# Softmax of the first batch with tokens on partitions, and another order of the opening, in an attention and MLP kernel on one core

## The chip, the cores and the metric

The kernel runs on one core of a Trainium2 chip. The metric is the device time of one execution in microseconds. Five engines work side by side, each through a queue of its own in order: TensorE (PE, matrix products into the PSUM memory), VectorE (DVE), ScalarE (ACT), GpSimd (POOL) and SyncE (SP), which here issues the loads. An instruction waits at the head of its queue until semaphores say that its inputs and its buffer are ready, and everything behind it in that queue waits too.

## The reference, cut to what matters

```python
def _attn_ref(q, k, v, phi):          # q, k, v: 8 x 8 x 576 x 64, phi: 8 x 8 x 576 x 32
    a = phi - np.max(phi, axis=2, keepdims=True)
    a = np.exp(a)
    a = a / (np.sum(a, axis=2, keepdims=True) + 1e-09)
    k_m = np.einsum('bhsm,bhsd->bhmd', a, k)
    v_m = np.einsum('bhsm,bhsd->bhmd', a, v)
    scores = scale * np.matmul(q, k_m.transpose(0, 1, 3, 2))
    scores = scores - np.max(scores, axis=-1, keepdims=True)
    attn = np.exp(scores)
    attn = attn / (np.sum(attn, axis=-1, keepdims=True) + 1e-09)
    return np.matmul(attn, v_m)
def _moe_ref(x, w_in, w_out):         # x: 4608 x 512, w_in: 512 x 2048, w_out: 2048 x 512
    h = x @ w_in
    g = h - np.tanh(h)
    return g @ w_out
```

Each of the 8 batches has 8 heads with a memory of 32 rows: `k_m` and `v_m` are 32 x 64 for each head, and the softmax of a token runs over 32 scores for each head. The weights come as 64-bit floats.

## The kernel before, in words

**Staging.** The product `attn @ v_m @ w_in` is taken as `attn @ P`, where `P = v_m @ w_in` is made once for each batch and each of four blocks `fb` of 512 columns of `w_in` (the word `P`, function `att_p`). The 4608 tokens are cut into 18 units `u` of 256. For each unit and block, `mm1` (word `H`, L723) makes `h` from `P` and the weights of attention, a row of elementwise steps makes `g` from `h`, and `mm2` (word `M`, L804) or `mm2_blocks` multiplies `g` by `w_out`. Precision comes from pairs of 16-bit numbers: each factor is split into a high and a low half (`ph` and the second half of its tile for P, which `att_pl` makes, `ah` and `al` for the attention weights, `win_hi` and `win_lo`, `wout_hi` and `wout_lo`), and each product is taken from three of the four combinations, so `mm1` takes 24 products for one unit of one batch.

**The weights.** `conv` (word `T`) turns a pair of 64-bit blocks into 32-bit floats: `tops` (the upper bits, `to_tops`, L524), then a shift and or on VectorE (`to_f32`, L532, tiles `wq` or `wt` by pair: pair 0 is `wq0`), then the high half (L564). `low` (`L`) or `low_pe` (`Lp`, a product on TensorE, tile `pw`) makes the low half. `P` of block 0 needs pairs 0 and 1, of block 1 pairs 2 and 3. The pair's raw blocks are `raw0` and `raw1`, and so on; blocks from 16 on are of `w_out`.

**Batch 0.** The scores are made with the 32 rows of the memory of 4 heads on the 128 partitions and the tokens along the columns (`scores`, L394, two tiles `t` of 288 tokens). VectorE turns them in squares of 32 by 32 (L403), so that a token's 32 scores lie along the columns; maximum (L422), difference (L424, on GpSimd), exponential (L427), sum (L433 to L435) and division (L437) follow, and VectorE turns the result back (L442) for the split into `ah` and `al` (`att_split`). `kT` is the turned `k_m`, `kvn` the pooled and normalised memory, `vh` and `vl` the halves of the turned `v_m`.

**Order.** All that happens until unit 4 stands in a table of words, `START`. Each word is a step or, for a function with `yield`, its next part; a word thus issues a few instructions, and the table fixes the order in every queue. `Z` issues two products on constant data that nobody reads (`warm`). `ENGINES` and `PLACES` give some steps to another engine or buffer. From unit 4 on a planner's slots follow. PSUM buffers are scarce: tag `pa` has one, tag `h` two; a tile of `pp` (P before its split) takes the `pa` buffer.

## Time and profile before

| what | value |
|---|---|
| runs | 640.74, 641.08, 643.17 us; median 641.08 us |
| the profiled execution | 641.09 us, of which the profile spans 639.3 us |
| TensorE products | 627.8 us busy, 98% of the span |
| VectorE, ScalarE, GpSimd | 523.9, 367.3, 260.7 us busy |

Busy time is a sum over engines that work at once, so the table says only which of them has no room left. The `warm` products are in TensorE's busy time too.

### The profile page before, as it was taken

The numbers are of one execution on the slowest core, as the hardware profiler recorded it, in microseconds if no ns is written. First come the engines' busy times: TensorE is split into PE (matmuls) and PEld (weight loads), VectorE is DVE, ScalarE is ACT, GpSimd is POOL, SyncE is SP. The second block draws the span as 40 slices with busy tenths as digits, with TensorE's granted clock in tenths as the row PEclk, the third lists the DMA queues.
The fourth block names the chain that finished last, engine by engine and source line by source line (L and its number), as shares of the span: only waits on it lengthen the run. The fifth ranks groups of instructions, "written<-read, shape, count | busy, mean of one in ns | idle before, by whom it ended". The sixth has DMA issues, their size and how long they took to land.

```text
span 639.3 us, 15482 instructions
## 1 busy us (share of the span) xinstructions
PE 627.8 (98%) x6658; PEld 453.3 (71%) x6658; DVE 523.9 (82%) x755; ACT 367.3 (57%) x491; POOL 260.7 (41%) x179
## 2 busy tenths in 40 slices
...
GB/s 322 377 415 319 274 55 249 38 150 122 48 63 105 169 3 89 44 159 149 108 79 115 173 87 62 153 174 36 107 158 141 100 111 121 87 101 124 87 35 38
DMA packets 28156, 85.50 MB, mean 134 GB/s; under 512 B 3632, under 2 KB 4400, under 8 KB 27568
## 3 DMA queue, kind: packets, MB, share of 16 engines
...
q14 instruction: 22, 0.18, 0.1%
...
## 4 chain that ended last, share of the span: by engine, by line
PE 70%; DVE 9%; issue 7%; ACT 6%; POOL 4%; DMA 1%; SPq 0%; ACTq 0%; POOLq 0%; DVEq 0%
PE hs L723 16%; PE x L870 11%; PE o L863 9%; PE o L804 9%; PE o L870 7%; PE h L723 7%; PE o1h L804 3%; DVE f L772 3%; PE pp L684 3%; PE pkv L354 2%; ACT u L730 2%; POOL g L759 2%; DVE h L748 2%; DVE h L738 2%; DMA raws<-in_w_in_dram 1%
## 5 line engine op out<-in xcount | busy, mean ns | idle before, releaser
L759 POOL TENSOR_TENSOR g<-h,g 128x1024 f16<-128x1024 f32 x64 | 140.9, 2202 | 301.6 <-ACT g L114 174.7
L723 PEld LDWEIGHTS <-ph 128*128 128x128 f16 x2304 | 177.6, 98 | 20.2 <-issue 4.1
L723 PE MATMUL hs<-ah,ph 128*128 128x256 f16 (+3 forms) x1152 | 151.4, 246 | 0.0
L723 PE MATMUL hs<-al,ph 128*128 128x256 f16 (+3 forms) x576 | 127.6, 246 | 0.0
L743 ACT ACTIVATE u<-u,beta 128x1024 f32<-128x1024 f32 x72 | 82.5, 1148 | 76.3 <-DVE h L738 76.3
L114 ACT ACTIVATE g<-h 128x1024 f16<-128x1024 f32 x64 | 67.6, 1056 | 101.1 <-DVE h L748 97.1
L738 DVE SCALAR_TENSOR_TENSOR h<-hs,u 128x1024 f32<-128x1024 f32 x54 | 65.8, 1219 | 72.9 <-ACT u L730 72.1
L863 PE MATMUL o<-wout_hi,g 128*128 128x512 f16 x432 | 104.6, 379 | 0.0
L870 PEld LDWEIGHTS <-f 128*128 128x128 f16 x896 | 87.7, 98 | 10.1
L748 DVE SCALAR_TENSOR_TENSOR h<-u,h 128x1024 f32<-128x1024 f32 x72 | 88.4, 1228 | 4.5 <-ACT u L743 4.4
L870 PEld LDWEIGHTS <-g 128*128 128x128 f16 x672 | 64.2, 98 | 27.3 <-issue 6.0
L870 PE MATMUL x<-bt,f 128*128 128x256 f16 x672 | 82.5, 273 | 0.0
L804 PEld LDWEIGHTS <-g 128*128 128x128 f16 x384 | 36.7, 98 | 47.2 <-issue 2.6
L863 PEld LDWEIGHTS <-g 128*128 128x128 f16 x432 | 41.2, 98 | 40.1 <-issue 3.8
L772 DVE TENSOR_TENSOR f<-g 128x512 f16<-128x512 f16 x112 | 68.3, 650 | 1.7
L730 ACT ACTIVATE u<-hs 128x1024 f32<-128x1024 f32 x54 | 54.8, 1016 | 23.1 <-PE hs L723 20.4
L804 PE MATMUL o<-wout_hi,g 128*128 128x512 f16 x192 | 58.8, 379 | 0.6 <-ACT g L114 0.6
L723 PE MATMUL h<-ah,ph 128*128 128x256 f16 (+3 forms) x384 | 50.4, 246 | 0.7 <-DVE ph L702 0.7
L723 PE MATMUL h<-al,ph 128*128 128x256 f16 (+2 forms) x192 | 42.5, 246 | 0.0
L804 PE MATMUL o<-wout_lo,g 128*128 128x512 f16 x96 | 36.4, 379 | 0.0
L599 POOL TENSOR_TENSOR fy<-chk 128x512 f32<-128x512 f32 x32 | 33.7, 1067 | 0.0
L870 PE MATMUL o<-bt,g 128*128 128x256 f16 x224 | 33.6, 273 | 0.0
...
## 6 DMA issues: line engine op xcount, KB each, us to landing
...
```

The lines of the kernel that those rows point to most:

```text
L114: nc.scalar.activation(o, x, AF.Copy, scale=1.0 if scale is None else scale)
L599: nc.gpsimd.tensor_tensor(y, hf, hf, op=ALU.mult)
L723: nc.tensor.matmul(hp[:, k, tu : tu + w], px[:, g, cs], d[ax][:, g, ta : ta + w], start=(n == 0), stop=(n == 5),)
L730: nc.scalar.activation(uu, hp, AF.Square, scale=1.0 / (S_A * S_P))
L738: nc.vector.scalar_tensor_tensor(h3, hp, C2 * S_G / (S_A * S_P), uu, op0=ALU.mult, op1=ALU.mult)
L743: nc.scalar.activation(uu, uu, AF.Square, bias=c["beta"])
L748: nc.vector.scalar_tensor_tensor(h3, uu, CC, hp, op0=ALU.add, op1=ALU.mult)
L759: (eng or on(nc, f"gl{u}_{fb}", "g")).tensor_tensor(gg[:, 1], h3, gg[:, 0], op=ALU.subtract)
L772: nc.vector.tensor_tensor(o, x, y, op=op)
L804: nc.tensor.matmul(o, gx[:, k, P * tt : P * tt + P], wx[:, 4 * fb + k, :], start=(first and k == 0 and wx is wout_hi and gx is gh), stop=( ...
L863: nc.tensor.matmul(o[th], gg[:, 0, k, P * th : P * th + P], wout_hi[:, 4 * fb + k, :], start=(first and k == 0), stop=False)
L870: nc.tensor.matmul(dst, a(1 - n, kk), b(n, kk), start=(new and kk == 0 and n == 0), stop=(end and kk == 1 and n == 1))
```

## The change

For batch 0 alone the scores come out with tokens on the partitions (`rows_scores`): the queries of a head are the stationary factor, 128 tokens at a time, and the moving factor is `k2`, a tile of 64 columns for each head in which the memories of the two heads of a pair stand in two diagonal blocks. Tile 0 holds 512 columns (tokens 0 to 255), tile 1 holds 640. The two turns on VectorE before and the two behind the softmax are gone: maximum and difference (both on VectorE now) read PSUM, the division is on VectorE, and TensorE turns the weights (`rows_turn`) into PSUM, from where `ah` and `al` are made. The queries of batch 0 come in another layout from the host (`qa`).

P of batch 0, blocks 0 and 1, is made from 32-bit factors in one go (`p_exact`: 8 products in place of 24); it needs neither the low halves nor the high ones. `v_m` is kept in 32 bits for that (`vT0`).

`START` stands in another order, and steps of the first units change engines and buffers. `conv` issues shift and high half one word earlier. Three more `Z` stand in the table. The diff, cut:

```diff
 START = """
-FX0 KK01 KK00 XR00 XR01 Z00 YX00 YX01 XT00 i4:kv2 Q00 XT00 Q01 KV00 XT01 XT01 XT01 Z00 VK00 KV01 VK01 i3:gg i2:gg NK0
...
+FX0 Z00 XR00 XR01 YX00 XT00 YX01 KK01 Z00 XT01 Z00 XT00 KK00 i2:gg XT01 XT01 i3:gg Q00 VK00 VK01 Q01 NK0 T01 Z00 Z00
...
 ENGINE_LIST = """
-g: hi11 lo10 lo11 lo12 lo13 lo14 lo4 lo5 lo6 lo8 sc11 sc14 tops13 tops2 tops8
-v: ah21 al00 al10 al21 div10 div20 e01 e10 el0 gh0_3 gh1_2 gh1_3 gh2_1 gh2_2 gh3_1 gh3_2 gh4_0 gl0_0 gl0_1 gl0_2
...
+g: hi1 hi12 hi6 lo1 lo10 lo11 lo12 lo13 lo14 lo5 lo6 lo7 sc11 sc14 sc6 sc7 tops1 tops11 tops13 tops15 tops3 tops8
+v: ah20 al10 al21 div00 div01 div10 div11 div20 e01 e10 el0 gh1_2 gh1_3 gh2_3 gh3_1 gh4_0 gh4_1 gl0_0 gl1_2 gl1_3
...
 PLACE_LIST = """
-0: raw18 g11 g03 h340
...
+2: g31
 """
...
+EXACT = tuple((0, fb) for fb in (0, 1,))
...
         yield
-        d["kT"] = self.big.tile([P, 128], F32, tag="kT", name="kT0", bufs=1)
-        cast(self.tc, self.c, "kT0", "a", d["kT"], pa)
+        k2, pa = self.k2, pa.rearrange("p (h m) -> p h m", m=32)
+        cast(self.tc, self.c, "kT0", "a", k2[0:64, :, 0], pa[0:64])
+        nc.vector.tensor_copy(k2[64:P, :, 1], pa[64:P])
...
-        self.tc.nc.sync.dma_start(x, self.ins["qt"][b, t])
+        self.tc.nc.sync.dma_start(x, self.ins["qt"][b, t] if b else self.ins["qa"][t])
...
+    def rows_scores(self, d, t, ps):
+
+        nc, k2 = self.tc.nc, self.k2
+        pa = ps[0].tile([P, 512], F32, tag="o1", name="psc00") if t == 0 else self.psum("psc01", ps[1]).rearrange("p a x -> p (a x)")
+        d["ps", t] = pa
+        for c in range(2):
+            px = pa[:, 256 * c : 256 * c + 256].rearrange("p (r h m) -> p h r m", r=2, h=4)
+            for h in range(4):
+                nc.tensor.matmul(px[:, h], d["q", h, t][:, P * c : P * c + P], k2[:, h], start=True, stop=True)
+        if t == 0:
+            return
+        for j in range(2):
+            for r in range(2):
+                rs, os = slice(64 * r, 64 * r + 64), slice(64 * r + 32 * j, 64 * r + 32 * j + 32)
+                for h in range(4):
+                    nc.tensor.matmul(
+                        pa[os, 512 + 32 * h : 544 + 32 * h], d["q", h, j][rs, 256:HS], k2[rs, h, r], start=True, stop=True
+                    )
+
+    def rows_max(self, d, t):
+
+        nc, big, n, o = self.tc.nc, self.big, (512, 640)[t], 512 * t
+        if t == 0:
+            d["sc"] = big.tile([P, S * 2], F32, tag="sc", name="sc0")
+        p3 = d["ps", t][:, 0:n].rearrange("p (n m) -> p n m", m=32)
+        d["s", t] = s = d["sc"][:, o : o + n]
+        d["s3", t] = s3 = s.rearrange("p (n m) -> p n m", m=32)
+        m = big.tile([P, n // 32], F32, tag="sm", name=f"sm0{t}")
+        nc.vector.tensor_reduce(m, p3, axis=AX.X, op=ALU.max)
+        yield
+        nc.vector.tensor_tensor(s3, p3, m.unsqueeze(2).to_broadcast((P, n // 32, 32)), op=ALU.subtract)
+
+    def rows_turn(self, d, t, ps):
+
+        nc, s, ident = self.tc.nc, d["s", t], self.c["ident"]
+        if t == 0:
+            pa = ps[0].tile([P, 512], F32, tag="o1", name="pat0").rearrange("p (r x) -> p r x", r=2)
+        else:
+            pa = self.psum("pat1", ps[1])
+        for c in range(2):
+            for r in range(2):
+                o = 256 * c + P * r
+                nc.tensor.transpose(pa[:, r, P * c : P * c + P], s[:, o : o + P], ident)
+        for r in range(2 * t):
+            rs = slice(64 * r, 64 * r + 64)
+            nc.tensor.matmul(pa[:, r, 256:320], s[rs, 512:640], ident[rs, rs], start=True, stop=True)
+        d["ps", t] = pa[:, :, 0 : 256 + 64 * t]
...
-        nc, NB, s3 = self.tc.nc, HS // 16, d["s3", t]
+        nc, s3 = self.tc.nc, d["s3", t]
+        NB = HS // 16 if b else 16 + 4 * t
...
+    att.k2 = big.tile([P, 4, 2, 32], F32, tag="kvn", name="k2")
+    nc.gpsimd.memset(att.k2, 0)
...
         to_f32(p, y, ts)
+        t = ts[0].bitcast(F32).rearrange("p (i f) -> p i f", i=2) if len(ts) == 1 else None
+        tfs[p] = [t[:, i] for i in range(2)] if len(ts) == 1 else [t.bitcast(F32) for t in ts]
         tops.append(y)
         yield
-        yield
         his[p] = half_of(p, win_hi, wout_hi)
-        if len(ts) == 1:
-            t = ts[0].bitcast(F32).rearrange("p (i f) -> p i f", i=2)
-            tfs[p], todo = [t[:, i] for i in range(2)], [(his[p], t)]
-        else:
-            tfs[p] = [t.bitcast(F32) for t in ts]
-            todo = [(his[p][:, i], tfs[p][i]) for i in range(2)]
+        todo = [(his[p], t)] if len(ts) == 1 else [(his[p][:, i], tfs[p][i]) for i in range(2)]
         for o, x in todo:
...
         pv = d["pv"]
-        d["vh"] = big.tile([P, 128], F16, tag="vh", name=f"vh{b}", bufs=3)
-        d["vl"] = big.tile([P, 128], F16, tag="vl", name=f"vl{b}", bufs=3)
         d["p"] = [None] * NFB
+        if b == 0:
+            d["v"] = big.tile([P, 128], F32, tag="vT", name="vT0", bufs=1)
+            cast(tc, c, "vf0", "a", d["v"], pv)
+            yield
+        d["vh"] = big.tile([P, 128], F16, tag="vh", name=f"vh{b}", bufs=2)
+        d["vl"] = big.tile([P, 128], F16, tag="vl", name=f"vl{b}", bufs=2)
         cast(tc, c, f"vh{b}", "a", d["vh"], pv, S_V)
         yield
...
+        if b == 0:
+            ts, pa = slice(256 * t, 256 + 320 * t), d["ps", t]
+            nc.scalar.activation(d["ah"][:, :, ts], pa, AF.Copy)
+            yield
+            nc.vector.tensor_tensor(d["al"][:, :, ts], pa, d["ah"][:, :, ts], op=ALU.subtract)
+            return
...
+
+    def p_exact(fb, pa):
+        for h in range(4):
+            w = tfs[2 * fb + h // 2][h % 2]
+            for r in range(2):
+                rs = slice(64 * r, 64 * r + 64)
+                nc.tensor.matmul(
+                    pa[32 * h : 32 * h + 32, r, :], st[0]["v"][rs, 32 * h : 32 * h + 32], w[rs], start=True, stop=True
+                )
+
+    def p_scale(b, fb):
+        return S_P if (b, fb) in EXACT else S_P / (S_V * S_W)
...
-        p_terms(b, fb, pa, True)
+        p_exact(fb, pa) if (b, fb) in EXACT else p_terms(b, fb, pa, True)
...
         pp = big.tile([P, 2, 2, 512], F16, tag=P_TAG[b, fb], name=f"ph{b}{fb}", bufs=1)
...
-        cast(tc, c, f"ph{b}{fb}", "a", ph, pa, sc)
+        cast(tc, c, f"ph{b}{fb}", "a", ph, pa, p_scale(b, fb))
...
-        nc.vector.scalar_tensor_tensor(pl, pa, S_P / (S_V * S_W), ph, op0=ALU.mult, op1=ALU.subtract)
+        nc.vector.scalar_tensor_tensor(pl, pa, p_scale(b, fb), ph, op0=ALU.mult, op1=ALU.subtract)
...
-        if u == 0:
-            ots = big.tile([P, 2, DM], F32, tag="uu", name=f"ot{u}")
         for tt in range(2):
-            ot = ots[:, tt] if u == 0 else pr.tile([P, DM], F32, tag="pr", name=f"ot{u}{tt}")
+            ot = pr.tile([P, DM], F32, tag="pr", name=f"ot{u}{tt}")
...
-        "S": lambda b, t: att.scores(b, st[b], t, early(b) if t or b == 0 else None),
-        "AM": lambda b, t: att.soft_max(b, st[b], t), "AE": lambda b, t: att.soft_exp(b, st[b], t), "AD": lambda b, t: att.soft_div(b, st[b], t, S_A),
-        "AT": lambda b, t: att.soft_turn(b, st[b], t), "AS": att_split,
+        "S": lambda b, t: att.scores(b, st[b], t, early(b) if t or b == 0 else None) if b else att.rows_scores(st[0], t, (ps_o, ps_early)),
+        "AM": lambda b, t: att.soft_max(b, st[b], t) if b else att.rows_max(st[0], t), "AE": lambda b, t: att.soft_exp(b, st[b], t), "AD": lambda b, t: att.soft_div(b, st[b], t, S_A),
+        "AT": lambda b, t: att.soft_turn(b, st[b], t) if b else att.rows_turn(st[0], t, (ps_o, ps_early)), "AS": att_split,
...
+    qa = q[0].reshape(4, 2, S, D).transpose(1, 3, 0, 2).reshape(P, 4, S)
+    qa = np.stack([np.concatenate([qa[:, :, 256 * t : 256 * t + 256], qa[:, :, 512 + 32 * t : 544 + 32 * t]], axis=2) for t in range(2)])
```

**What moves.** The first place is ScalarE's queue behind the first exponential of batch 0 (`sc0` are the scores, `vy` sums for a check on the range, `vT0` the 32-bit copy of `v_m`). Before:

```order
L427 ACTIVATE sc0_238<-sc0_238 128x576
L114 ACTIVATE win_hi_101<-wt20_253 128x512
L114 ACTIVATE win_hi_101<-wt21_254 128x512
L427 ACTIVATE sc0_238<-sc0_238 128x576
L114 ACTIVATE tops1_107<-raw2_211 128x512
L114 ACTIVATE tops1_107<-raw3_209 128x512
L114 ACTIVATE tops0_105<-raw0_218 128x512
L114 ACTIVATE tops0_105<-raw1_220 128x512
L114 ACTIVATE vh0_355<-pk0_167 128x128
L114 ACTIVATE ah0_362<-af0_335 128x2x288
```

Now:

```order
L477 ACTIVATE sc0_270<-sc0_270 128x512
L477 ACTIVATE sc0_270<-sc0_270 128x640
L717 ACTIVATE vy00_341,stat_67<-kvn0_214 128x64
L717 ACTIVATE vy01_343,stat_67<-kvn0_214 128x64
L115 ACTIVATE tops1_109<-raws4_294 128x1024
L727 ACTIVATE ah0_360<-pat0_354 128x2x256
L115 ACTIVATE vT0_363<-pk0_168 128x128
L115 ACTIVATE win_hi_101<-wt20_387 128x512
```

The two exponentials follow each other; behind them come the sums for the check, the upper bits of pair 2 (`raws4`), the first `ah` and then `vT0`. In VectorE's queue the cast to `vh0` now waits for `vT0` and stands ahead of the second division.

The second place is VectorE's queue from the conversion of pair 1 (before) and from the second division (now) to the split of the first P (the line that writes `ph00`). Before:

```order
L532 SCALAR_TENSOR_TENSOR wq1_338<-raw2_211,tops1_107 128x512
L532 SCALAR_TENSOR_TENSOR wq1_338<-raw3_209,tops1_107 128x512
L442 STREAM_TRANSPOSE af0_335<-sc0_238 128x576
L532 SCALAR_TENSOR_TENSOR wq0_352<-raw0_218,tops0_105 128x512
L532 SCALAR_TENSOR_TENSOR wq0_352<-raw1_220,tops0_105 128x512
L118 TENSOR_SCALAR win_hi_101<-wq1_338 128x512 x2
L658 SCALAR_TENSOR_TENSOR vl0_356<-pk0_167,vh0_355 128x128
L584 SCALAR_TENSOR_TENSOR win_lo_102<-wq1_338,win_hi_101 128x512 x2
L532 SCALAR_TENSOR_TENSOR wq3_377<-raws6_239,tops0_105 128x1024
L118 TENSOR_SCALAR win_hi_101<-wq3_377 128x2x512
L675 TENSOR_TENSOR al0_363<-af0_335,ah0_362 128x2x288
L702 SCALAR_TENSOR_TENSOR ph00_420<-pp00_387,ph00_420 128x1024
```

Now:

```order
L488 TENSOR_TENSOR sc0_270<-sc0_270,sz01_350 128x640
L711 SCALAR_TENSOR_TENSOR vl0_374<-pk0_168,vh0_373 128x128
L585 SCALAR_TENSOR_TENSOR wt20_387<-raws4_294,tops1_109 128x512
L585 SCALAR_TENSOR_TENSOR wt21_388<-raws4_294,tops1_109 128x512
L117 CAST tops0_107<-raw0_297 128x512
L117 CAST tops0_107<-raw1_306 128x512
L585 SCALAR_TENSOR_TENSOR wq0_401<-raw0_297,tops0_107 128x512
L585 SCALAR_TENSOR_TENSOR wq0_401<-raw1_306,tops0_107 128x512
L729 TENSOR_TENSOR al0_361<-pat0_354,ah0_360 128x2x256
L729 TENSOR_TENSOR al0_361<-pat1_379,ah0_360 128x2x320
L772 SCALAR_TENSOR_TENSOR ph00_420<-pp00_406,ph00_420 128x1024
L585 SCALAR_TENSOR_TENSOR wq3_423<-raws6_331,tops1_109 128x1024
```

Pair 0 (`wq0`) now stands behind the whole softmax, behind pair 2 (`wt20`, `wt21`) and behind its own two `tops` casts, which ScalarE made before. `wq3` (pair 3) now stands behind the split of the first P.

The third place is TensorE's queue ahead of the first product of unit 0 (`h00`). Before:

```order
L684 LDWEIGHTS vh0_355
L684 MATMUL pp00_387<-win_lo_102,vh0_355 32x512
L590 MATMUL pw3_424<-wq3_377,idw_63 128x512
L591 LDWEIGHTS nid16_65
L591 MATMUL pw3_424<-win_hi_101,nid16_65 128x512
L590 MATMUL pw3_424<-wq3_377,idw_63 128x512
L591 LDWEIGHTS nid16_65
L591 MATMUL pw3_424<-win_hi_101,nid16_65 128x512
L723 LDWEIGHTS ph00_420
L723 MATMUL h00_451<-ah0_362,ph00_420 128x256
```

Now:

```order
L640 MATMUL pw0_429<-win_hi_101,nid16_65 128x512
L1036 LDWEIGHTS w16_66
L1036 MATMUL warm_111<-w16_66 128x512
L1036 LDWEIGHTS w16_66
L1036 MATMUL warm_111<-w16_66 128x512
L741 MATMUL pp01_445<-wt20_387,vT0_363 32x512 x2
L741 MATMUL pp01_445<-wt21_388,vT0_363 32x512 x2
L741 MATMUL pp01_445<-wq3_423,vT0_363 32x512 x4
L793 LDWEIGHTS ph00_420
L793 MATMUL h00_454<-ah0_360,ph00_420 128x256
```

Ahead of `h00` stood a low half, `pw3`, and now stands the second P, `pp01`, whose last four products read `wq3`. `pw3` now follows `h00`. `pp01` shares a PSUM buffer with `pp00`, and so it waits until `ph00` is split in full.

## Rows read from the trace of the kernel before

**Rows 1.** Timeline of TensorE, opening: start us, busy us, engine, line, instruction, count, [idle before].
```profile
7.32 0.63 PE L334 MATMUL pet<-ident,pt 128*128 128x128 f32 x4 [1.01 <-issue]
7.88 0.43 PE L335 MATMUL pel<-ident,pt 128*64 128x128 f32 x2
...
9.19 0.60 PE L968 MATMUL warm<-w 128*128 128x512 f16 x2
...
10.33 0.32 PE L208 MATMUL pk<-kt,e 64*32 64x65 f32 x8
...
13.26 0.72 PE L394 MATMUL psc<-q,kT 64*32 64x288 f32 x16 [0.57 <-DMA q<-in_qt_dram]
```

**Rows 2.** The same timeline, where the main products of the first units start.
```profile
28.70 1.13 PE L590 MATMUL pw<-wq,idw 128*128 128x512 f32 x2
...
31.02 0.27 PE L723 MATMUL h<-ah,ph 128*128 128x256 f16 x1
...
32.05 0.39 PE L723 MATMUL h<-ah,ph 128*128 128x256 f16 x2 [0.65 <-DVE ph L702]
...
34.56 0.41 PE L684 MATMUL pp<-win_hi,vh 64*32 64x512 f16 x8
...
40.93 1.98 PE L354 MATMUL pkv<-kv,e 128*32 128x129 f32 x64 [0.51 <-ACT e L114]
```

**Rows 3.** The chain that ended last, one link: start us, us, what.
```profile
35.40 2.73 PE h L723 x24
```

**Rows 4.** Timeline of TensorE at two later places.
```profile
82.61 0.39 PE L804 MATMUL o<-wout_hi,g 128*128 128x512 f16 x1 [0.56 <-ACT g L114]
...
184.09 0.23 PE L723 MATMUL hs<-ah,ph 128*128 128x128 f16 x1
```

**Rows 5.** Stretches: PE, PEld, DVE, ACT, POOL busy (instructions), PE clock, DMA share, GB/s.
```profile
15.00:16.00 1.00, 1.00 (x17) 0.13 (x2) 0.97 (x3) 0.00 (x0) 0.00 (x0) 0.50 1.03 399
200.00:300.00 100.00, 100.00 (x1114) 76.78 (x1112) 74.53 (x120) 50.27 (x66) 35.65 (x21) 1.00 0.28 98
```

**Rows 6.** Groups by line: busy us, mean ns of one.
```profile
L334 PE MATMUL pet<-ident,pt 128*128 128x128 f32 x16 | 2.6, 282 | 1.0 <-issue 1.0
...
L442 DVE STREAM_TRANSPOSE af<-sc 128x576 f32<-128x576 f32 x16 | 12.3, 767 | 0.0
...
L403 DVE STREAM_TRANSPOSE sc<-psc 128x576 f32<-128x576 f32 x12 | 9.2, 770 | 0.6 <-PE psc L394 0.6
```

**Rows 7.** Timeline of VectorE.
```profile
17.99 0.75 DVE L433 TENSOR_REDUCE sz<-sc 128x18 f32<-128x576 f32 x1 [0.49 <-ACT sc L427]
...
21.45 0.25 DVE L217 TENSOR_TENSOR kvn<-pk,kr 128x128 f32<-128x128 f32 x1
21.62 1.72 DVE L532 SCALAR_TENSOR_TENSOR wq<-raw,tops 128x512 uint32<-128x512 uint32 x2
...
23.96 1.25 DVE L532 SCALAR_TENSOR_TENSOR wq<-raw,tops 128x512 uint32<-128x512 uint32 x2
...
30.78 1.21 DVE L702 SCALAR_TENSOR_TENSOR ph<-pp,ph 128x1024 f16<-128x1024 f32 x1
...
34.44 0.80 DVE L116 CAST tops<-raw 128x512 f16<-128x512 bf16 x2
```

**Rows 8.** Timeline of ScalarE.
```profile
12.72 0.28 ACT L114 ACTIVATE kT<-ptr 128x128 f32<-128x128 f32 x1 [4.14 <-PE ptr L224]
...
18.90 0.67 ACT L427 ACTIVATE sc<-sc 128x576 f32<-128x576 f32 x1
...
23.22 0.78 ACT L114 ACTIVATE tops<-raw 128x512 f16<-128x512 bf16 x1 [0.49 <-DMA raw<-in_w_in_dram]
...
25.79 1.35 ACT L114 ACTIVATE tops<-raws 128x1024 f16<-128x1024 bf16 x1
...
28.84 1.02 ACT L114 ACTIVATE ph<-pp 128x1024 f16<-128x1024 f32 x1
...
51.07 0.24 ACT L664 ACTIVATE vy<-kvn 128x64 f32<-128x64 f32 x1
```

More of the change, by code (lines that the diff above doesn't have):

```diff
@@ new lines @@
+Z00 UU0 o6:gg W0 o7:gg Z00 AD00 AD01 AT00 T02 AS00 UV0 Z00 Z00 FX1 o0:gg UV0 Z00 AD01 AT01 UV0 T02 T02 Lp02 AS01 T00
+T00 T00 P00 AS00 T01 AS01 T03 P00 PL00 T03 XR10 Z00 Lp00 T11 Lp00 T11 T11 Z00 P01 H00 T03 P01 Lp02 KB1 H00 XR11 L11
+o1:gg KA1 YX10 o2:gg YX11 o3:gg T08 PL01 Lp03 XT10 T08 XT11 Lp03 XT10 ap00 H10 XT11 XT11 V10 V11 L01 T08 H10 ap00 a10
+H11 L01 i10:kv3 Q10 ap00 T09 N1 U1 o4:gg T09 a10 o5:gg H01 T09 Q11 ap00 a10 L09 i8:kv2 UV1 L09 L08 U1 T05 UV1 H11 S10
+T10 H01 L08 c00 S10 T10 a10 T05 T10 L11 a11 AM10 a11 L10 i14:kv3 M00 c10 AM10 ap01 Q20 S11 L10 M10 FA2 a11 ap01 S11
```

41 lines of the change are left out of this document (18 added, 23 removed).

## The prediction

> **What bounds the kernel now.** I read the totals first: TensorE is busy 98% of the span, no other engine above 82%. Then the stretches: between 200 and 300 us TensorE has no gap, at the full granted clock, in the last of [rows 5]. Then TensorE's timeline for its gaps. Ahead of 32.05 us there are many waits; behind, only two that belong to this change's stretch: 0.51 us ahead of the first product for batch 1's memory at 40.93 [rows 2], and 0.56 us at 82.61 [rows 4]. The chain of waits agrees: from the first product of `h` it is mostly TensorE itself [rows 3]. So the end of the kernel is the start of `h00`, plus TensorE's work behind it. From 184.09 on (unit 4) [rows 4] both kernels follow the same list of slots; what counts happens before.
>
> **The sum's frame.** I call X the time at which `h00` starts and runs through. Before, two of its 24 products ran early at 31.02 and the rest from 32.05 [rows 2]; a link of 24 takes 2.73 [rows 3], so one takes 0.11, and X was 32.05 - 0.22 = 31.83. Behind `h00` the change takes from TensorE: `pp01` (34.56 to 35.40, 0.8) [rows 2, 3]; two `warm` products, 0.6 as the pair at 9.19 [rows 1]; the 0.51 at 40.93, since batch 1's memory and another product of `h` have changed places; and, if the new order also covers it, the 0.56 at 82.61. It adds `pw3`, which now follows `h00`: the first half of such a low half starts at 28.70, and the four products end at 31.02 [rows 2], so 2.3. Net: 0.8 + 0.6 + 0.51 + 0.56 - 2.3 = 0.2 us less work. So the kernel is as fast as before if X is 31.83 + 0.2 = 32.0, and every microsecond of X beyond is one of time.
>
> **What the change removes.** On the path to `h00` stood two turns from PSUM and two back, 0.77 each [rows 6], and subtraction and division on GpSimd. It also removes three low or high halves ahead of P. But in its place stands a new chain, which I now walk.
>
> **Scores.** `kT` was ready at 12.72 + 0.28 = 13.00 [rows 8] and the queries let the scores start at 13.26 [rows 1]. Now a further `warm` pair (0.6) lies ahead on TensorE, and the second half of `k2` is a copy on VectorE, priced as the small `kvn` step, 0.25 [rows 7], and partly beside ScalarE's half. I take 13.95 (bounds 13.3 and 14.2). Each tile takes 8 products in 32-bit with 128 stationary columns and 64 moving; a 32-bit product leaves two records, so 16. Before, a stationary factor was 32 columns wide, four products lay side by side, and 16 records took 0.72 [rows 1]. The new ones fill the array and cannot lie side by side. The nearest rows are the turns `pet`: four records of 128 by 128 in 32-bit, 0.63 in all with 0.282 for one [rows 1, 6], so (0.63 - 0.282) / 3 = 0.116 from one to the next. That makes 16 x 0.116 = 1.86 for a tile: `psc00` ends at 15.8. The lower bound is 256 column-passes at full clock, 0.11 for a product as in `h` [rows 3], so 0.9 a tile; the upper one is a pair of `pel` at 0.43 [rows 1], so 3.4. I choose the middle one, being the same size of stationary factor and type. `psc01` has the same plus 16 small products, about 0.06 each (eight records at 10.33 take 0.32) [rows 1]: 2.9, ending at 18.8.
>
> **Softmax.** VectorE's price is 0.75 for 576 columns [rows 7], so 0.67 for tile 0 and 0.83 for tile 1. The chain behind 18.8: maximum 1 to 19.7, then (it stands ahead in the queue) sum 0 and its small steps 1.2, to 20.9; difference 1 to 21.8; exponential 1 on ScalarE, 0.74 from 0.67 [rows 8], to 22.55. On ScalarE follow two sums for the check (0.24 each [rows 8], with their waits 0.7) to 23.25, upper bits of pair 2, 1.35 [rows 8], to 24.6, `ah` 0.6 to 25.2, `vT0` 0.28 to 25.5. `vh0` on VectorE waits for `vT0`, though division 1, right behind it in the queue, was ready: 0.25 to 25.75. What is queued behind this wait is division 1 and the whole of pair 2, then pair 0.
>
> **From there to P.** Division 1, 0.83, `vl0` 0.25, pair 2 1.25 [rows 7], the two `tops` casts 0.80, `wq0` 1.25 [rows 7]: 30.15. Independent neighbours on VectorE overlap by some 0.08 (one row ends at 21.70, and the next starts at 21.62 [rows 7]), over seven of them 0.6: `wq0` ends at 29.5. Before, it ended at 25.2 [rows 7]. `pp00` from 32-bit factors: a 32-bit product of 512 columns takes about 0.9 (1.13 less the 0.2 by which a lone row outlasts its spacing [rows 2]); the eight lie side by side, as the eight of `pp` do, which also take 0.41 [rows 2]. So 30.4. Then `ph` 1.02 [rows 8] to 31.45, and `pl` 1.21 [rows 7] to 32.7.
>
> **The new wait.** `pp01` stands ahead of `h00` in TensorE's queue. It needs `pp00`'s buffer, free at 32.7, and `wq3`, which stands behind `pl` on VectorE: 1.2 as a conversion of 1024 columns (two of 512 take 1.25 [rows 7]), so 33.85. Its last four products take 0.9: **X = 34.8**, 2.8 later than the break-even of 32.0. `pw3` behind `h00` waits for the eviction of `pw2` on ScalarE, two evictions of 1.02 [rows 8] after `pp01`, and is hidden by `h00`'s 2.7.
>
> **Costed at nothing.** GpSimd gets some 12 us more work up to unit 4 and VectorE loses 6; the cover is TensorE, full behind `h00`, and half of GpSimd's time is idle. The queue of SP: its load of a later block of `w_out` waits for `wq0`'s buffer and holds the loads behind it back by 1 to 2 us; unit 0's second stage, which needs them, has some 17 us of products ahead of it. If that cover is gone, up to 1 us. The clock: it fell to 0.50 between 15 and 16 us, after a pause in the scores [rows 5], and I count no such fall for the new scores, since nothing interrupts the two tiles.
>
> [...] The turn from PSUM took 770 ns and the turn from SBUF 767 [rows 6]: I price PSUM operands as SBUF's. [...]
>
> **Sum.** The profiled execution took 641.09 us, which is the median of the runs within 0.01. 641.09 + 2.8 = **643.9 us**. A measurement of this kernel can tell about 0.5%, 3.2 us, from no change: 637.9 to 644.3.
>
> **Rivals.**
> (a) Fast scores. If a score product costs its columns alone, 0.11, each tile takes 0.9, the softmax comes 2.1 us earlier, and X = 32.7: 641.8 us. For it: the main products of 256 columns do run at 0.11 [rows 3]. Against: no 32-bit product with a stationary factor of 128 columns does here. Chance 0.2.
> (b) Slower scores, by over 0.5%. The 16 records of a tile are spaced wider, as `pel` (0.43 for two [rows 1]), or lie at the half clock, which the chip did grant at 15 us [rows 5]. Each 0.01 us per record is 0.32 us over both tiles, so it decides from 0.13 per record; at 0.18, X = 36.9: 646.0 us. For it: the clock's fall came right behind the scores before. Chance 0.22.
> (c) Faster floor. If softmax and `vT0` don't bind at all, the loads still do: pair 3's raw block is there at 25.79, its upper bits take 1.35 [rows 8], `wq3` 1.2, `pp01` 0.9: X = 29.3 and 638.4 us. Against: it takes VectorE's queue out of order. Chance 0.05, and even this is within 0.5%.
> (d) Something I did not see: 0.03.
> My forecast, X between 33.6 and 35.9, has 0.5, its own range being 642.7 to 645.0.
>
> **How the numbers follow.** The forecast's upper part (0.16) lies above 644.3; with (b) that is 0.38 for slower. Faster by over 0.5% is the lower edge of (c) with half of (d), 0.03. The rest, 0.59, is within. The range for 8 in 10 reaches from (a) with a little room, 640.6, to (b)'s price, 646.4.
>
> **What would show it.** In the changed kernel's trace: the scores' records at 0.116 from one to the next, the two tiles ending at 15.8 and 18.8 at full clock; `vT0` ending at 25.5 with VectorE idle in front of `vh0`; `wq0` ending at 29.5; `pp01` starting behind `pl` at 32.7 and waiting for `wq3`; `h00` at 34.8 in one piece; unit 4's first `hs` at 184.09 + 2.8 = 186.9. The prediction is wrong if `h00` starts before 33.6 or after 35.9, or if stalls of more than 1 us stand behind it: then a queue that I counted as covered (SP's loads, GpSimd's `tops`) was not.

## The result, and the profile after

Timed side by side, the changed kernel took 647.09 us (four runs, 646.46 to 647.27) and the kernel before 641.02: the ratio is 1.008, 95% interval 1.0063 to 1.0098. That is slower by 0.8%, the side of the bound to which the prediction gave 0.38, not the "within 0.5%" to which it gave 0.59. The ratio times the 641.08 on which the prediction was built is 646.2, in the top end of its range (640.6 to 646.4); the bare median is 0.7 us above the range, and both are above the forecast's own 645.0. The profiled execution took 646.46 us, its span is 644.3, 5.0 more than before.

Where the 5.0 us lie is read from two places. `h00` starts at 35.22, against an effective 31.83 before: 3.39. Unit 4's first `hs`, behind which both kernels run the same slots, starts at 189.16 against 184.09 [rows 4]: 5.07. So two thirds of the loss is ahead of `h00`, 1.68 us lie between `h00` and unit 4, and none behind.

TensorE's timeline of the changed kernel (columns as in [rows 1]), the rows that answer to [rows 1, 2, 4]:

```profile
13.27 3.79 PE L415 MATMUL psc<-k,q 128*128 128x64 f32 x32 [0.32 <-DVE k L232]
16.98 0.90 PE L422 MATMUL psc<-k,q 64*32 64x32 f32 x32
...
28.79 1.59 PE L741 MATMUL pp<-wq,vT 64*32 64x512 f32 x16 [0.50 <-DVE wq L585]
...
33.43 1.06 PE L741 MATMUL pp<-wt,vT 64*32 64x512 f32 x8
34.23 1.06 PE L741 MATMUL pp<-wq,vT 64*32 64x512 f32 x8
35.22 0.28 PE L793 MATMUL h<-ah,ph 128*128 128x256 f16 x1
...
37.85 1.02 PE L639 MATMUL pw<-wq,idw 128*128 128x512 f32 x2
...
47.57 0.27 PE L793 MATMUL h<-ah,ph 128*128 128x256 f16 x1 [0.63 <-DVE h L808]
...
189.16 0.23 PE L793 MATMUL hs<-ah,ph 128*128 128x128 f16 x1
```

A score record takes 0.275 by itself, so the 32 are (3.79 - 0.275) / 31 = 0.113 apart, with nothing in between; the row of `pp00` and the two of `pp01` show the 32-bit P; `h00` starts when the last `pp01` product is issued; `pw3` follows, as forecast; and there is one long new wait, 0.63 at 47.57. The weight loads show what spaces the score products:

```profile
13.26 3.65 PEld L415 LDWEIGHTS psc<-k,q 128*128 128x128 f32 x32 [0.81 <-DVE k L232]
```

A load takes 0.19 by itself, so the 32 are (3.65 - 0.19) / 31 = 0.112 apart: they follow one another without a pause, at the pace of the products. VectorE's timeline, which answers to [rows 7]:

```profile
17.91 0.82 DVE L435 TENSOR_REDUCE sm<-psc 128x20 f32<-128x640 f32 x1 [1.20 <-PE psc L422]
...
21.31 0.82 DVE L484 TENSOR_REDUCE sz<-sc 128x20 f32<-128x640 f32 x1
...
23.78 0.29 DVE L119 TENSOR_SCALAR vh<-pk 128x128 f16<-128x128 f32 x1 [1.12 <-ACT vT L115]
...
26.12 1.96 DVE L117 CAST tops<-raw 128x512 f16<-128x512 bf16 x2
27.98 1.27 DVE L585 SCALAR_TENSOR_TENSOR wq<-raw,tops 128x512 uint32<-128x512 uint32 x2
...
31.52 1.23 DVE L772 SCALAR_TENSOR_TENSOR ph<-pp,ph 128x1024 f16<-128x1024 f32 x1 [0.94 <-ACT ph L115]
32.95 1.23 DVE L585 SCALAR_TENSOR_TENSOR wq<-raws,tops 128x1024 uint32<-128x1024 uint32 x1 [0.20 <-PE pw L639]
...
40.05 1.82 DVE L585 SCALAR_TENSOR_TENSOR wq<-raw,tops 128x512 uint32<-128x512 uint32 x2 [1.54 <-POOL tops L117]
...
42.40 1.22 DVE L808 SCALAR_TENSOR_TENSOR h<-h,u 128x1024 f32<-128x1024 f32 x1
```

To be seen: the wait of 1.12 in front of `vh0`; two `tops` casts that take 1.96, where two of the same size took 0.80 before [rows 7]; `wq0` ending at 29.25; and a conversion at 40.05 that waits 1.54 for GpSimd. The sum over 640 columns reads SBUF and the maximum over 640 reads PSUM: both 0.82. ScalarE's timeline, which answers to [rows 8], with `vT0` behind the sums for the check, the upper bits of pair 2 and the first `ah`:

```profile
20.54 0.74 ACT L477 ACTIVATE sc<-sc 128x640 f32<-128x640 f32 x1 [3.16 <-DVE sc L437]
...
21.80 1.34 ACT L115 ACTIVATE tops<-raws 128x1024 f16<-128x1024 bf16 x1
23.01 0.57 ACT L727 ACTIVATE ah<-pat 128x512 f16<-128x512 f32 x1
23.48 0.27 ACT L115 ACTIVATE vT<-pk 128x128 f32<-128x128 f32 x1
...
30.47 1.02 ACT L115 ACTIVATE ph<-pp 128x1024 f16<-128x1024 f32 x1 [0.55 <-PE pp L741]
```

GpSimd's timeline, with the cast that runs beside VectorE's two casts, and the late one for pair 8:

```profile
26.32 1.44 POOL L117 CAST tops<-raws 128x1024 f16<-128x1024 bf16 x1 [9.89 <-ACT win_hi L115]
...
40.01 0.77 POOL L117 CAST tops<-raw 128x512 f16<-128x512 bf16 x1 [0.70 <-DMA raw<-in_w_out_dram]
```

And the queue of SP (start of an issue, and the time from there to the end of the last one in the row): of two loads of `w_out` the first goes through at 15.96, the second only at 28.67.

```profile
15.96 13.04 SPq L546 DMA_DIRECT2D raw<-in_w_out_dram  x2
28.67 0.33 SPq L546 DMA_DIRECT2D raw<-in_w_out_dram  x1
```

Before, SP stood still too, but its next issue started at 22.77:

```profile
22.77 0.93 SPq L493 DMA_DIRECT2D raw<-in_w_out_dram  x2
```

### The profile page after: what moved, and what is told of

Read it like the earlier page. It is cut to its first block, busy times and chain, and to the rows that moved or that the text cites. A ratio compares the mean times of both kernels' runs of the same rounds, so it can differ in the third digit from the quotient of the medians.

```text
span 644.3 us, 15577 instructions
## 1 busy us (share of the span) xinstructions
PE 634.5 (98%) x6692; PEld 458.3 (71%) x6692; DVE 517.8 (80%) x750; ACT 365.1 (57%) x484; POOL 273.4 (42%) x190
## 4 chain that ended last, share of the span: by engine, by line
PE 69%; DVE 9%; issue 7%; ACT 6%; POOL 5%; DMA 2%; SPq 0%; ACTq 0%; POOLq 0%; DVEq 0%
PE hs L793 17%; PE x L938 12%; PE o L931 10%; PE o L938 8%; PE o L874 7%; PE h L793 4%; POOL g L829 2%; PE pp L755 2%; DVE h L818 2%; ACT u L800 2%; PE pkv L356 2%; DVE f L842 2%; PE warm L1036 1%; DVE h L808 1%; DMA raw<-in_w_out_dram 1%
## 5 line engine op out<-in xcount | busy, mean ns | idle before, releaser
L829 POOL TENSOR_TENSOR g<-h,g 128x1024 f16<-128x1024 f32 x66 | 143.6, 2175 | 293.0 <-ACT g L115 196.8
L115 ACT ACTIVATE g<-h 128x1024 f16<-128x1024 f32 x66 | 69.7, 1056 | 108.6 <-DVE h L818 105.8
```

Of the source, the lines that this page charges most:

```text
L115: nc.scalar.activation(o, x, AF.Copy, scale=1.0 if scale is None else scale)
L829: (eng or on(nc, f"gl{u}_{fb}", "g")).tensor_tensor(gg[:, 1], h3, gg[:, 0], op=ALU.subtract)
```

## The experiments

The twelve runs are read at the same places: start of the scores, start of `h00` (X), unit 4's first `hs`, and what the transfers moved from 12 to 60 us. Openings differ by up to 0.6 us from one execution to the next (the scores start between 13.17 and 13.76), so small differences are counted from the start of the scores. X and `hs` come from one profile for each run. The ratio is to the kernel before, timed on the same chip; the intervals of e1 to e8 and of e11 overlap that of the changed kernel, those of e9, e10 and e12 lie below it.

| run | scores start, us | X, us | first `hs`, us | MB from 12 to 60 us | ratio, 95% interval |
|---|---|---|---|---|---|
| before | 13.26 | 31.83 | 184.09 | 19.21 | 1 |
| changed | 13.27 | 35.22 | 189.16 | 14.98 | 1.008 (1.0063 to 1.0098) |
| e1 | 13.24 | 33.88 | 188.42 | 15.32 | 1.005 (1.003 to 1.007) |
| e2 | 13.24 | 34.06 | 187.69 | 15.44 | 1.0064 (1.0046 to 1.0082) |
| e3 | 13.24 | 34.17 | 191.87 | 14.93 | 1.0108 (1.0076 to 1.014) |
| e4 | 13.31 | 35.25 | 189.12 | 15.02 | 1.0088 (1.0055 to 1.0121) |
| e5 | 13.52 | 36.10 | 189.62 | 15.02 | 1.0105 (1.0073 to 1.0138) |
| e6 | 13.43 | 35.80 | 190.03 | 14.97 | 1.0074 (1.0051 to 1.0097) |
| e7 | 13.63 | 37.38 | 191.09 | 14.98 | 1.0103 (1.0086 to 1.0119) |
| e8 | 13.35 | 32.90 | 190.76 | 14.99 | 1.0101 (1.0082 to 1.0119) |
| e9 | 13.76 | 33.30 | 187.65 | 15.64 | 1.0039 (1.0027 to 1.0051) |
| e10 | 13.17 | 32.71 | 186.10 | 16.04 | 1.003 (1.0017 to 1.0043) |
| e11 | 13.31 | 33.46 | 188.60 | 15.29 | 1.006 (1.0046 to 1.0074) |
| e12 | 13.53 | 31.35 | 185.73 | 16.49 | 1.0018 (1.0008 to 1.0027) |

**e1: `vT0` early.** In `START`:

```diff
-AT00 T02 AS00 UV0 Z00 Z00 FX1
+AT00 UV0 T02 AS00 Z00 Z00 FX1
```

> The copy to vT0 stands ahead of pair 2's upper bits and of the first ah in ScalarE's queue; nothing else moves. Chain theory (everything from the softmax to P is one chain through VectorE, and the 1.12 us for which VectorE stood idle in front of vh0 is on it): vT0 ends at 22.1 instead of 23.75, wq0 ends 1.1 us earlier, at 28.15, h00 starts at 34.1 instead of 35.22, unit 4's first hs at 188.1 instead of 189.16, and the time falls by 1.1 us. Rival (another wait, a load or the upper bits of pair 2, ends last there): h00 within 0.3 us of 35.22, no change.

X came 1.34 earlier, the wait in front of `vh0` gone; the rival is out. But `hs` came only 0.74 earlier. VectorE's timeline shows that the loss moved on with GpSimd's cast (25.16 to 26.80 here): now the conversion `wq0` takes 2.40 (1.27 in the changed kernel), and the `tops` casts are back at 0.80.

```profile
24.82 0.80 DVE L117 CAST tops<-raw 128x512 f16<-128x512 bf16 x2
25.50 2.40 DVE L585 SCALAR_TENSOR_TENSOR wq<-raw,tops 128x512 uint32<-128x512 uint32 x2
```

**e2: upper bits of pair 3 on VectorE.** In `ENGINE_LIST`:

```diff
-g: ... tops13 tops15 tops3 tops8
+g: ... tops13 tops15 tops8
-v: ... tops0 vh0
+v: ... tops0 tops3 vh0
```

> The upper bits of pair 3 are cast on VectorE instead of GpSimd, behind the first al; nothing else moves. Contention theory (VectorE's two casts to tops0 took 0.98 us each instead of 0.40 because GpSimd cast at the same time): the pair takes 0.8 instead of 1.96 us, wq0 ends at 28.1 instead of 29.25, h00 starts 1.0 to 1.2 us earlier, and the time falls by 1 us; the cast itself falls into the 0.94 us for which VectorE waited for ph00. Rival (the two casts are slow by themselves, or wait for the load of raw1): they stay at 1.9 us or more, the added cast of 0.8 or more delays wq3, and h00 starts 0 to 0.5 us later.

With no cast on GpSimd beside them the casts take 0.79 and the conversion 1.30 in VectorE's timeline, and X came 1.16 earlier. The contention is shown: alone 0.79, beside GpSimd's cast 1.96.

```profile
26.09 0.79 DVE L117 CAST tops<-raw 128x512 f16<-128x512 bf16 x2
26.76 1.30 DVE L585 SCALAR_TENSOR_TENSOR wq<-raw,tops 128x512 uint32<-128x512 uint32 x2
```

**e3: `pp01` behind `h00`.**

```diff
-Z00 P01 H00 T03 P01
+Z00 H00 P01 T03 P01
```

> P of block 1 stands behind the first products of unit 0 in TensorE's queue. Theory of the prediction's new wait (pp01 waiting for wq3 is what holds h00): h00 starts when pl is done, at 32.8 to 33.0 instead of 35.22, but the 1.8 us of pp01 then follow it, so that unit 4's first hs comes 0.4 to 0.6 us earlier: the wait itself is worth little, because TensorE had real work in it. Rival A (the wait is the cause of the loss): hs 2.2 us earlier and the time back to about 645. Rival B (pw3 and pw2 need the PSUM buffers in the old order): a new stall behind h00, and hs no earlier or later than 189.16.

Rival B. `h00` waits for the eviction of `pw0` (its PSUM buffer) until 34.17, not 33; `pp01` starts 3.45 us later, and `pw3` behind it waits 2.15 for another eviction: `hs` 2.7 later. TensorE's timeline:

```profile
34.17 0.27 PE L793 MATMUL h<-ah,ph 128*128 128x256 f16 x1 [0.68 <-ACT win_lo L115]
...
36.88 0.63 PE L741 MATMUL pp<-wt,vT 64*32 64x512 f32 x4
...
40.12 1.12 PE L639 MATMUL pw<-wq,idw 128*128 128x512 f32 x2 [2.15 <-ACT win_lo L115]
```

**e4: first step of `h00` ahead of pair 8 on VectorE.**

```diff
-T08 PL01 Lp03 XT10 T08 XT11 Lp03 XT10 ap00 H10
+T08 PL01 Lp03 XT10 ap00 T08 XT11 Lp03 XT10 H10
```

> The first elementwise step of h00 stands ahead of the conversion of pair 8 in VectorE's queue, which waits for late loads of w_out. Theory (the loads of w_out are late since SP stood behind wq0's buffer until 29.1, pair 8 is converted late, and what stands behind it in VectorE's queue is late too: this is the 0.63 us stall of TensorE at 47.57): h00's step runs at 39.1 instead of 42.4, the stall goes, and hs comes 0.6 us earlier, at 188.5. Rival (another buffer or engine releases it at the same time): the stall moves to a neighbour, and hs stays within 0.2 us of 189.16.

The step ran at 39.14 as expected, and nothing was gained: TensorE's wait stands at 48.01 now, for unit 1's step, whose input ScalarE makes behind pair 8's high half.

```profile
48.01 0.27 PE L793 MATMUL h<-ah,ph 128*128 128x256 f16 x1 [1.05 <-DVE h L808]
```

**e5: low half of pair 3 on VectorE.**

```diff
-T08 PL01 Lp03 XT10 T08 XT11 Lp03 XT10 ap00 H10
+T08 PL01 L03 L03 XT10 T08 XT11 XT10 ap00 H10
```

> The low half of pair 3 is made on VectorE (two subtractions, 1.3 us) behind the split of P of block 1, where VectorE waits 1.54 us for pair 8, instead of by TensorE's four products pw3 behind h00; nothing else moves. Theory (TensorE is full behind h00, so the 2.16 us of pw3, which stood ahead of h00 in a hole before the change, are paid in full): h00 still at 35.2, unit 4's first hs 2.1 us earlier, at 187.0, the time 2.1 us less. Rival (behind h00 the elementwise steps of the first units and the loads bind, so TensorE's freed time turns into waits): the stall at 47.57 grows by the same, and hs comes less than 0.7 us earlier.

The rival holds. 2.16 us of TensorE's work are gone from behind `h00`, and a wait of 1.78 for batch 1's exponent stands there instead (TensorE's timeline):

```profile
40.67 0.65 PE L336 MATMUL pet<-ident,pt 128*128 128x128 f32 x4 [1.78 <-ACT pt L323]
```

X is no measure here: it is 0.9 later, 0.6 if counted from the start of the scores, for a reason ahead of the edit. In this execution the granted clock went from 1.00 to 0.50 between 26 and 30 us, behind a wait of 1.58 that the changed kernel has too, where it stayed at 1.00. The stretches, columns as in [rows 5]:

```profile
27.00:28.00 1.00, 1.00 (x3) 0.43 (x2) 1.00 (x1) 0.72 (x2) 1.00 (x1) 0.50 0.00 0
```

**e6: pair 0 ahead of pair 2.** In `START`, with the low half of pair 2 behind `pp00`:

```diff
-UV0 T02 T02 Lp02 AS01 T00 T00 T00 P00 AS00 T01 AS01 T03 P00 PL00 T03 XR10 Z00 Lp00 T11 Lp00
+UV0 T00 T00 T02 AS01 P00 AS00 T00 T01 AS01 T03 P00 Lp00 T02 PL00 T03 XR10 Z00 Lp02 T11 Lp00
```

> Pair 0 is converted ahead of pair 2 on VectorE, pp00 stands ahead of pw2 on TensorE, and ScalarE makes the high half of pair 0 and ph00 ahead of the high half of pair 2. Chain theory: wq0 ends at 27.0 instead of 29.25 (1.28 for pair 2 and 1.16 since GpSimd's cast then comes later than VectorE's), pp00 at 28.0, pl at 30.6, wq3 (behind pw0) at 31.7, h00 at 33.4 instead of 35.22; since TensorE's work is the same and only waits go, unit 4's first hs comes 1.0 to 1.8 us earlier. Rival (the loads of w_in, not the order on VectorE, end last: raw1 or raws6): wq0 not before 28.5 and h00 less than 0.7 us earlier.

`wq0` ended at 27.04, so no load holds it, and that rival is out. But X was later, by 0.4 counted from the start of the scores. TensorE's timeline: `pp00` took 2.46 at the clock of 0.50 (1.59 in the changed kernel), the first half of `pw0` behind it 1.58 (1.02), and `pp01` stood behind `pw2` to 34.78 though `wq3` was there at 32.95. From `pp00` to `h00` TensorE had no pause, so the clock cost 0.87 + 0.56 = 1.4 us there; without it X would have come about 1 us earlier than in the changed kernel (an estimate from these rows, if no other wait had taken its place). The run does not decide what the order is worth: its one execution with a mean granted clock of 1.000 took 645.03 us, the three with 0.997 took 646.38 to 647.54.

```profile
26.58 2.46 PE L741 MATMUL pp<-wq,vT 64*32 64x512 f32 x16 [0.47 <-DVE wq L585]
28.97 1.58 PE L639 MATMUL pw<-wq,idw 128*128 128x512 f32 x2
...
32.11 1.02 PE L639 MATMUL pw<-wt,idw 128*128 128x512 f32 x2
```

**e7: eight score products twice.**

```diff
-            for h in range(4):
+            for h in [*range(4)] * (1 + t):
```

> The eight 128-column score products of tile 1 are made twice (the same values into the same place), 16 records more at 0.118 us, 1.9 us of TensorE's time. Chain theory (the second tile's scores stand at the head of the one chain to h00): the maximum of tile 1 starts 1.9 later, at 19.8 instead of 17.91, vT0, wq0 and h00 (37.1 instead of 35.22) all 1.9 later, hs at 191.0, the time 1.9 us more. Rival (the loads or the conversions of w_in bind there, and the softmax has slack): h00 less than 1 us later, with the difference taken from VectorE's waits.

TensorE's timeline has 48 records in 5.57. That is 1.78 more. X came 2.16 later and `hs` 1.93; counted from the start of the scores 1.80 and 1.57: what the scores take longer goes through to X in full and to `hs` for the most part.

```profile
13.63 5.57 PE L415 MATMUL psc<-k,q 128*128 128x64 f32 x48 [0.32 <-DVE k L232]
```

**e8: four edits.** e1, e2, `L03` as in e5, and pair 8 behind the first steps of units 0 and 1:

```diff
-T08 PL01 Lp03 XT10 T08 XT11 Lp03 XT10 ap00 H10 XT11 XT11 V10 V11 L01 T08 H10 ap00 a10
+T08 PL01 XT10 XT11 XT10 ap00 H10 L03 L03 XT11 XT11 V10 V11 L01 H10 ap00 T08 T08 a10
```

> Four edits together: vT0 early, the upper bits of pair 3 on VectorE, the low half of pair 3 on VectorE, and pair 8 behind the first steps of unit 0 and 1. If the losses add up (0.74 and 1.47 as measured in unit 4's first hs, 2.1 for pw3, 0.6 for the stall at 47.57), hs comes 4.9 us earlier, at 184.3, where it was before the change (184.09), and the time is within 0.1% of before. If they hide one another (one chain, of which each edit takes the same piece), hs stays above 186 and the time above 643.5.

`hs` stayed above 186, as in the second case, but not for its reason: from the start of the scores X was 2.4 earlier than in the changed kernel, the sum of both early edits, and yet `hs` came 1.6 later. Behind `h00` TensorE waited 1.78 for batch 1's exponent and 1.89 for a step of `h`, and the clock was at 0.50 behind both waits (38 to 42 and 48 to 52 us). These account for the late end, roughly: the waits are 3.0 more than the 0.63 of the changed kernel, and some 7 us at half the clock cost about 3.5 (an estimate: behind the first wait the products of `h` are 0.21 apart at 0.50, and 0.11 at 1.00), against 2.16 of `pw3` saved; from `h00` to `hs` it took 3.9 longer.

```profile
37.47 0.66 PE L336 MATMUL pet<-ident,pt 128*128 128x128 f32 x4 [1.78 <-ACT pt L323]
...
47.90 0.27 PE L793 MATMUL h<-ah,ph 128*128 128x256 f16 x1 [1.89 <-DVE h L808]
```

**e9: e1 and e2 together.** Their two diffs.

> The two edits that helped, together: vT0 early on ScalarE, and the upper bits of pair 3 on VectorE. Chain theory (both shorten the same chain at different places, VectorE's wait of 1.12 us in front of vh0 and its casts that took 1.16 us too long): h00 starts at 32.9 to 33.1, 2.2 us earlier than in the changed kernel, and with pw3 still behind h00 unit 4's first hs comes 1.8 to 2.4 us earlier, at 187.0; the time is 2 us under the changed kernel's, ratio to before 1.004 to 1.006. Rival (behind h00 another chain, batch 1's exponent or the loads of w_out, ends last): h00 at 33 all the same, but hs not earlier than the 187.7 of the second edit alone.

From the start of the scores to `h00` 19.54 instead of 21.95: the two edits add up ahead of `h00` (2.41; alone 1.31 and 1.13). `hs` stands at 187.65, as with e2 alone, but here the scores started 0.52 later; counted from there `hs` is 2.00 earlier than in the changed kernel, and 0.71 and 1.44 with the edits alone. So they add up there too, within what one profile tells, and the ratio is the lowest of the three, though the intervals touch: the chain theory, not the rival.

**e10: unit 1's products where `pw3` stood.** e9, and:

```diff
-T03 XR10 Z00 Lp00 T11 Lp00 T11 T11 Z00 P01 H00 T03 P01 Lp02 KB1 H00 XR11 L11
-o1:gg KA1 YX10 o2:gg YX11 o3:gg T08 PL01 Lp03 XT10 T08 XT11 Lp03 XT10 ap00 H10 XT11 XT11 V10 V11 L01 T08 H10 ap00 a10
+T03 XR10 XR11 Z00 Lp00 T11 Lp00 T11 T11 Z00 P01 H00 T03 P01 Lp02 YX10 KB1 YX11 H00 H10 L11
+o1:gg KA1 o2:gg o3:gg T08 PL01 ap00 L03 L03 XT10 H10 XT10 ap00 XT11 T08 XT11 XT11 V10 V11 L01 T08 a10
```

> On top of those two: the low half of pair 3 on VectorE instead of pw3; batch 1's maximum and exponent ahead of the first elementwise step of unit 0 on ScalarE; and the products of unit 1 (h10) directly behind h00 on TensorE, where pw3 stood, with the first steps of units 0 and 1 ahead of pair 8 on VectorE. Theory from the last runs (taking pw3 away turned into a wait of 1.78 us for batch 1's exponent, because ScalarE had it behind h00; with products of h in its place TensorE has work there): h00 at 33, no wait over 1 us between h00 and 60 us, and hs at 184 to 185; time within 0.3% of before on either side. Rival (the two buffers of tag h, or the late loads of w_out, stop h01 or the first second-stage product instead): one wait of 1.5 us or more between 40 and 60 us, hs later than 186.5.

Between the two: 3.06 earlier at `hs`, the best of the runs that do all the work, and still 0.3% slower than before. TensorE's longest wait behind `h00` is 1.30, for ScalarE.

**e11: half of the score products.**

```diff
-            for h in range(4):
-                nc.tensor.matmul(px[:, h], d["q", h, t][:, P * c : P * c + P], k2[:, h], start=True, stop=True)
+            for h in range(0, 4, 2):
+                nc.tensor.matmul(px[:, h : h + 2], d["q", h, t][:, P * c : P * c + P], k2[:, h : h + 2], start=True, stop=True)
```

> In the changed kernel, each score product takes the columns of two heads at once from one head's queries, so half of the 128-column score products are left out, and the scores of every second head are those of wrong queries; all else is the same work. Four products instead of eight a tile. Chain theory (a score product is bound by its stationary factor, two records of 0.118 us whatever is moved, and the scores head the one chain to h00): 32 records for both tiles become 16, 1.9 us less; vT0, wq0 and h00 come 1.9 us earlier (h00 at 33.3), unit 4's first hs 1.3 to 1.9 us earlier. Rival A (a product of twice the columns takes twice the time): nothing moves. Rival B (the loads end last as soon as the scores are shorter): the second tile ends 1.9 us earlier but wq0 less than 1 us earlier.

16 records of twice the columns took 2.05, and their loads are as far apart as before, 0.111 (16 in 1.86): the stationary factor is the price, and rival A is out. X came 1.76 earlier (1.80 from the start of the scores). But `hs` only 0.56: the wait on a step of `h` grew from 0.63 to 1.55. That step is late because pair 8's second block is: GpSimd waits 1.99 for its load (0.70 in the changed kernel) and casts its upper bits at 39.54, only 0.47 earlier than there (40.01), though the load was issued 1.77 earlier (33.70 for 35.47).

```profile
13.31 2.05 PE L415 MATMUL psc<-k,q 128*128 128x128 f32 x16 [0.32 <-DVE k L232]
...
46.73 0.27 PE L793 MATMUL h<-ah,ph 128*128 128x256 f16 x1 [1.55 <-DVE h L808]
```

**e12: the same in e10.** The diff of e11 on that of e10.

> The same halved score products (the same part of the computation left out) in the kernel of the run with h10 behind h00. If the width of the score products is what is left of the loss there (hs at 186.10 against 184.09 before the change), hs comes to 184.2 to 184.8 and the time to within 0.15% of the kernel before. If the waits behind h00 (the loads of w_out and the steps on ScalarE and GpSimd) end last by then, h00 moves from 32.7 to about 31, hs stays above 185.3, and the time stays 0.2% or more above before.

The second case, with a time 0.18% above before where 0.2% or more was expected. `h00` starts at 31.35, ahead of the kernel before, and `hs` is 1.64 later than there. TensorE waits 1.31 for ScalarE; its products for batch 1's memory then take 3.55 instead of 1.98 [rows 2], at a granted clock of 0.50 from 41 to 43 us.

```profile
38.87 0.63 PE L336 MATMUL pet<-ident,pt 128*128 128x128 f32 x4 [1.31 <-ACT u L813]
...
40.18 3.55 PE L356 MATMUL pkv<-kv,e 128*32 128x129 f32 x64 [0.33 <-ACT e L115]
```

## Why the prediction held, and where it did not

**Held by luck, as a number.** The verdict missed. That 646.2 lies in the range is luck: the range reached so far up only because of rival (b), slower scores, which did not happen.

**The path to `h00`: right, by errors that cancel.** X was forecast at 34.8 and was 35.22. The scores started 0.68 earlier than I took, the price of a record was right (0.113 for 0.116), and e7 and e11 show that it is on the path in both directions: +1.78 us of products gave X +1.80 from the start of the scores, 1.74 less gave -1.80. Rivals (a) and (b) are out: not the columns, not a wider spacing, not the clock (1.00 from 13.27 to 18.00). e11 says why: the stationary factor, whose loads are 0.112 apart here and 0.111 there, with twice the moving columns. `vT0` ended at 23.75, 1.75 ahead of the walk, and the wait in front of `vh0` was there as named; e1 shows that it cost 1.3 at X. The casts lost 1.16 of it again. `pp00` (30.38) and `pl` (32.75) came within 0.1 of the walk, `wq3` (34.18) within 0.4.

**The step that was mis-sized there** is "the two `tops` casts 0.80": 1.96, since GpSimd cast at the same time. I took the price from a row where GpSimd was idle, and counted GpSimd's 12 us more work as covered by TensorE without looking at what it does to VectorE. e2 shows it: 1.1 at X.

**The step that failed** is "so the end of the kernel is the start of `h00`, plus TensorE's work behind it", with "costed at nothing" for SP's queue. My account of TensorE's work is good (`pw3` 2.16 more; `pp01` 0.77, the `warm` pair with its wait 1.11, and the wait at 82.61, which went, 0.56 less: -0.28), but `h00` to `hs` took 1.68 longer, so about 2.0 us of waits are new: 0.63 at 47.57, the others under 0.4 each. That is the prediction's own sign of being wrong (stalls of more than 1 us behind `h00`, here in sum): a queue counted as covered was not. TensorE was full there before because other things just kept up; that is no proof that they have room. e5 took 2.16 us of work away and got a wait for most of it, e4 moved a wait, and in e12 X is better than before and the end is not.

**What keeps up no longer: the loads, for the longest wait; for the rest, most likely.** The stretches of before, columns as in [rows 5], the last two being the share of the transfer engines and what they moved, in GB/s:

```profile
12.00:30.00 18.00, 15.25 (x171) 6.64 (x171) 15.95 (x28) 11.30 (x18) 7.44 (x7) 0.91 1.00 379
30.00:60.00 30.00, 28.84 (x298) 17.85 (x297) 27.61 (x38) 25.70 (x40) 15.22 (x14) 1.00 1.02 413
60.00:100.00 40.00, 39.44 (x440) 24.18 (x439) 38.07 (x47) 32.04 (x45) 18.55 (x12) 1.00 0.51 179
```

From 12 to 60 us before, the transfers never pause: 19.21 MB, 400 GB/s over the stretch. Such rows were open to me, and I read only TensorE's column. Now the changed kernel:

```profile
12.00:30.00 18.00, 15.61 (x198) 9.64 (x196) 13.86 (x27) 7.13 (x15) 5.08 (x4) 1.00 0.72 277
24.00:29.00 5.00, 3.55 (x16) 1.77 (x18) 5.00 (x9) 2.15 (x4) 1.73 (x2) 1.00 0.04 16
30.00:60.00 30.00, 29.37 (x286) 17.80 (x281) 24.57 (x34) 24.59 (x34) 10.94 (x10) 1.00 0.87 333
60.00:100.00 40.00, 39.77 (x407) 23.04 (x406) 36.82 (x45) 29.84 (x41) 24.09 (x17) 1.00 0.79 299
```

From 24 to 29 us next to nothing moves, since SP stands in front of the buffer of `raw0`, which the first half of `wq0` frees at about 28.6 (27.98 and half of 1.27). SP's waits from 12 to 40 us, the longest group (us in total, times, longest):

```profile
SPq L546 <- DVE wq L585: 10.3, 2, 7.9
```

By 60 us 4.2 MB fewer are there, and 60 to 100 us moves at 299 instead of 179 GB/s what had been there before. I had this as 1 to 2 us later with a cover of 17 us; the issue came 5.9 us later (28.67 for 22.77). The softmax's lateness is thus paid twice: in X, and in the loads of `w_out` behind `wq0`.

For one wait this can be followed: the product at 47.57 waits for unit 1's step of `h` (46.29), whose input ScalarE makes (45.24) behind pair 8's high half; that and the step ahead of it on ScalarE stand behind pair 8's conversion on VectorE (40.05), which waits 1.54 for GpSimd (casts at 38.55 and 40.01, the second behind a wait of 0.70 for its load). e11 confirms it: `h00` came 1.76 us earlier, the cast only 0.47, and the wait grew by 0.92. For the rest the table speaks only weakly. `hs` falls with the MB in e9, e10 and e12, but an earlier `wq0` both shortens the path and frees the buffer, so X falls there too; and e8's few MB are in part of its own making, since with pair 8 converted later SP stood still from 35.9 to 45.2. In e12:

```profile
12.00:30.00 18.00, 17.38 (x197) 9.17 (x199) 16.38 (x31) 8.87 (x17) 3.99 (x4) 1.00 0.93 361
30.00:60.00 30.00, 28.37 (x280) 18.52 (x273) 26.79 (x38) 26.24 (x37) 13.51 (x12) 0.94 0.91 333
```

Even there 2.7 MB are missing. That the loads cause the rest is argued, not shown: no run moved them alone, as a buffer of its own for one block of `w_out` would have done, and e12 lost time to the clock and to a wait for ScalarE as well, so how its last 1.6 us divide stays open.

**The rest.** `pp01` ahead of `h00` was named as the new wait; e3 shows that of the two places this is the better one. PSUM operands were priced as SBUF's, and that held: 0.82 from PSUM and 0.82 from SBUF over 640 columns. No run undid one part of the change alone (the softmax, P in 32 bits, the order), so what each part costs or saves is not shown.
